# q's shift row folded and summed by one matmul, Wo split into two parts, and the third modulation vector applied behind Wo's product

## The chip, the cores and the metric

The kernel runs on one core of a Trainium2 chip. The metric is the device time of one execution in microseconds (us). The core has a matrix engine (TensorE, PE in the profile; its loads of weights have a row of their own, PEld), a vector engine (VectorE, DVE), an engine for activations and copies (ScalarE, ACT), GpSimd (POOL) and SyncE (SP), which here issues loads. Each engine works its own list of instructions in order, and engines wait for each other by semaphores.

## The reference

One transformer block with modulation vectors made from a condition `c`, over S = 2048 tokens of D = 448 channels, in fp32:

```python
mod = (_silu(c) @ w_mod).reshape(c.shape[0], 6, 1, -1)
sa, ca, ga, sb, cb, gb = (mod[:, 0], ..., mod[:, 5])
h = _layernorm(x, axis=-1) * (1 + ca) + sa
x = x + ga * _A_ref(h, A_wqkv, A_wo)
h = _layernorm(x, axis=-1) * (1 + cb) + sb
x = x + gb * _B_ref(h, B_w1, B_b1, B_w2, B_b2)
```

`_A_ref` is linear attention with 16 heads of 28 channels: q, k, v = h @ wqkv; phi(t) = where(t > 0, t + 1, exp(t)) + 1e-6 of q and k; kv = sum over tokens of phi(k) v, z = sum of phi(k); o = phi(q) kv / (phi(q) z + 1e-6); and the result is o @ wo. `_B_ref` is an MLP across the tokens (2048 to 1792 and back, gelu between), with a layer norm ahead of it.

`ga`, the third modulation vector (`mods[2]` in the code), scales the channels of what Wo puts out. So it may stand on Wo's columns, or on any product that ends with Wo.

## The kernel before

**Numbers.** Nearly every fp32 operand is split into a high part in a shorter format (fp32r) and a low part, the rest; a product of two is then three matmuls, high by high, low by high and high by low. Where the code splits, ACT makes the high part and DVE the low one by a subtraction (`split`), or ACT writes the negative of the high part and a transfer issued by POOL adds the full tile to it (`pkl` of most tiles, L527, and the later pieces of W1). A few matmuls take fp32 operands unsplit; the profile shows such a one as two records.

**Stage A, by token tiles t = 0 to 15 of 128 tokens (to some 98 us).** For each tile, PE projects k (`kp`, ten matmuls, L432) and closes it with one more matmul, whose operands are the rows of the layer norm's statistics (`hl`, made from `rw`, a transposition of the tile `rowst` that DVE fills, L395, L398, L404) and of the weights' column sums (`wrow`, L439). ACT takes exp and relu (`ek`, `rk`), DVE makes phi(k) (`pk`), and it is split into `pkh` and `pkl`; the normalised tile `xn` is split into `xh` and `xl`. Four tiles later (`KV_LAG`) PE adds the outer product of xn and phi(k) to four banks (`cacc`, eleven matmuls, L554). From t = 10 a projection of q (`qp`, with `eq`, `rq` and `pq`) comes with each tile. Past t = 15 the last four outer products follow, and two matmuls that sum phi(k) (`zp`, from `zh` and `zl`).

q needs a row of its own in `wrow`: the product of sa with the weights, `row_part` (DVE, into the tile `accb`), summed over its partitions together with the negative column sums of the scaled weights. `row_sum(0)` is seven matmuls, `row_bias(0)` the one for `accb`, in fp32; both stand at the start of t = 9, and `row_out(0)` at its end writes the sums into `wrow`.

**Between the stages (98 to 112 us).** From `cacc` and `zb`, a copy of zp, DVE and ACT make four tiles `cs`; PE multiplies them with v's weights (`kvb`), DVE applies the mask of the heads (`kvm`), and PE multiplies it with Wo in four groups of 112 rows (`wp`, fp32, L968). Wo's rows had been multiplied by `mods[2]` on DVE, one group each at the end of t = 13, 14 and 15 and one behind (L779, L791). ACT copies wp to `wpg`; transfers gather it into `wpr`, which is split into `wph` and `wpl`.

**Then i = 0 to 20.** For each tile, DVE makes 1 / den from phi(q) and zb and scales phi(q) to `pn` (L836 to L850); PE transposes it (`tq`), ACT and DVE split that, PE multiplies with wph and wpl (`op`), and the second layer norm follows. Five tiles later, PE adds the tile to the MLP's first layer (`up`, with W1 in pieces `pr`, each split into `ph` and `pl`). The first eight pieces are split by ACT and DVE, the others by ACT and a transfer (`PIECE_DMA`). The rest of the first layer and the second layer, `y`, run to the end.

**Order.** The order is written out by hand: each engine works its instructions as the code has them. Tiles come from a pool of 74 slots and another of 27 (`slot`, `tslot`), handed out in the order of the code, and one that takes a used slot waits until its last reader is done. Eight banks hold PE's results.

## Time and profile before

| | us |
|---|---|
| three runs | 433.62, 434.19, 433.53 (median 433.62) |
| the profiled execution | 434.09 |
| its span, first to last instruction | 432.4 |
| PE busy | 427.9 (99%) |
| DVE busy | 365.1 (84%) |
| ACT busy | 278.9 (65%) |
| POOL busy | 120.1 (28%) |

A row of the timeline gives the start and the length of an instruction in us, the engine, the line, the operation, what it writes and reads, and in brackets how long the engine had been idle before it and who ended that. Matmuls overlap: one is listed with 0.36 us, but in a row of them the next starts 0.20 us later. So PE's cost is read from the distance of starts, or from the chain of waits, where a run of matmuls of one line is one row.

### The profile page before, as it was taken

The numbers are of one execution on the slowest core, as the hardware profiler recorded it, in microseconds if no ns is written. First come the engines' busy times: TensorE is split into PE (matmuls) and PEld (weight loads), VectorE is DVE, ScalarE is ACT, GpSimd is POOL, SyncE is SP. The second block draws the span as 40 slices with busy tenths as digits, with TensorE's granted clock in tenths as the row PEclk, the third lists the DMA queues.
The fourth block names the chain that finished last, engine by engine and source line by source line (L and its number), as shares of the span: only waits on it lengthen the run. The fifth ranks groups of instructions, "written<-read, shape, count | busy, mean of one in ns | idle before, by whom it ended". The sixth has DMA issues, their size and how long they took to land.

```text
span 432.4 us, 7216 instructions
## 1 busy us (share of the span) xinstructions
PE 427.9 (99%) x2331; PEld 398.0 (92%) x2331; DVE 365.1 (84%) x814; ACT 278.9 (65%) x595; POOL 120.1 (28%) x199
## 2 busy tenths in 40 slices
PE   8999999999999999999999999999999999999997
PEld 8888899999899999999999999999999999999996
DVE  4899987889899999998579695739799998898894
ACT  5799869658578899996755263537464664655550
POOL 4345444300026577775200000010113131132010
PEclk9999999999999999999999999999999999999999
DMA  8997997565300036354427461577379977986431
GB/s 282 385 337 162 239 264 162 89 206 193 86 1 0 26 74 148 74 125 97 145 85 244 142 212 50 166 203 210 79 193 214 207 159 159 214 170 144 85 46 41
DMA packets 63797, 66.14 MB, mean 153 GB/s; under 512 B 4816, under 2 KB 55312, under 8 KB 63760
## 3 DMA queue, kind: packets, MB, share of 16 engines
q1 hardware_dynamic: 54688, 50.90, 37.8%
q0 software_dynamic: 8784, 14.32, 20.8%
q10 hardware_dynamic: 288, 0.46, 0.4%
q8 instruction: 18, 0.29, 0.3%
q14 instruction: 19, 0.16, 0.1%
HBM read 46.30 MB, written 7.34 MB: 124 GB/s over the span
## 4 chain that ended last, share of the span: by engine, by line
PE 97%; DVE 1%; ACT 1%; issue 0%
PE y L1183 19%; PE up L951 10%; PE up L950 10%; PE up L952 10%; PE y L1184 9%; PE cacc L554 7%; PE qp L432 7%; PE op L893 7%; PE kp L432 6%; PE op L900 1%; PE warm L188 1%; PE tq L863 1%; PE qp L439 1%; PE kvb L818 1%; PE wp L968 1%; PE rowb L287 1%
## 5 line engine op out<-in xcount | busy, mean ns | idle before, releaser
L950 PE MATMUL up<-h2h,ph 128*128 128x448 f32 x224 | 81.2, 362 | 0.0
L951 PE MATMUL up<-h2l,ph 128*128 128x448 f32 x224 | 81.2, 362 | 0.0
L952 PE MATMUL up<-h2h,pl 128*128 128x448 f32 x224 | 80.8, 361 | 0.0
L1138 POOL DMA_DIRECT2D a<-a x16 | 14.2, 964 | 142.6 <-DMA pr<-in_B_w_dram 76.7
L950 PEld LDWEIGHTS up<-h2h,ph 128*128 128x128 f32 x224 | 42.0, 188 | 3.1
L952 PEld LDWEIGHTS up<-h2h,pl 128*128 128x128 f32 x224 | 41.9, 187 | 3.0
L951 PEld LDWEIGHTS up<-h2l,ph 128*128 128x128 f32 x224 | 42.0, 188 | 2.3
L84 DVE TENSOR_TENSOR pl<-pr,ph 128x512 fp32r<-128x512 f32 x46 | 30.7, 688 | 2.6 <-ACT ph L83 1.7
L1189 ACT ACTIVATE cc<-y 128x448 f32<-128x448 f32 x24 | 13.0, 546 | 26.7 <-PE y L1184 26.7
L1102 DVE TENSOR_TENSOR u<-u,mod 128x448 f32<-128x448 f32 x14 | 8.7, 623 | 23.0 <-ACT u L1101 22.8
L83 ACT ACTIVATE ph<-pr 128x512 fp32r<-128x512 f32 x46 | 27.6, 623 | 0.8 <-PE up L952 0.5
L1101 ACT ACTIVATE u<-up,b 128x448 f32<-128x448 f32 x14 | 8.8, 625 | 25.4 <-PE up L952 24.9
L432 PE MATMUL kp<-wh,hh 128*128 128x448 f32 x64 | 23.8, 377 | 0.0
L554 PE MATMUL cacc<-pkh,xh 128*128 128x448 f32 x64 | 23.6, 369 | 0.0
L432 PE MATMUL qp<-wh,hh 128*128 128x448 f32 x64 | 23.5, 368 | 0.0
L1203 POOL DMA_DIRECT2D out_dram<-yt x14 | 12.7, 909 | 37.3 <-DVE yt L1194 27.9
L843 POOL TENSOR_SCALAR den<-den 128x16 f32<-128x16 f32 x16 | 8.8, 548 | 44.2 <-DVE den L840 44.2
L554 PE MATMUL cacc<-pkl,xh 128*128 128x448 f32 x56 | 20.3, 362 | 0.0
L893 PE MATMUL op<-wph,pth 128*128 128x448 f32 x48 | 18.7, 390 | 0.0
L1144 DVE TENSOR_TENSOR a<-a,s 128x512 f32<-128x512 f32 (+1 forms) x32 | 18.5, 622 | 0.0
L83 ACT ACTIVATE s2h<-s 128x512 fp32r<-128x512 f32 (+1 forms) x16 | 8.3, 569 | 15.5 <-DVE s L1144 15.5
L1183 PE MATMUL y<-ub,a11h 128*128 128x448 f32 x56 | 18.2, 375 | 0.0
(235 smaller groups left out, 1383.7 us busy)
## 6 DMA issues: line engine op xcount, KB each, us to landing
pr<-in_B_w_dram SPq DMA_DIRECT2D x56, 256.0 KB, 3.1
a<-in_B_w_dram SPq DMA_DIRECT2D x32, 256.0 KB, 4.8
a<-in_B_w_dram SPq DMA_DIRECT2D x32, 192.0 KB, 4.7
xt<-in_xt_dram SPq DMA_DIRECT2D x16, 256.0 KB, 5.0
x<-in_A_x_dram SPq DMA_DIRECT2D x16, 224.0 KB, 5.0
wm<-in_B_wmod_dram SPq DMA_DIRECT2D x16, 196.0 KB, 5.2
out_dram<-x SPq DMA_DIRECT2D x14, 224.0 KB, 2.3
out_dram<-yt POOLq DMA_DIRECT2D x14, 224.0 KB, 6.1
```

What stands on the lines that cost most here:

```text
L83: nc.scalar.activation(hi, full, AF.Copy)
L84: nc.vector.tensor_sub(lo, full, hi.bitcast(F32))
L432: nc.tensor.matmul(pps[t, j][:, :D], a[:, ch * P:(ch + 1) * P], w, start=first, stop=False)
L554: nc.tensor.matmul(cacc[ch][:, :D], a[:, s], b, start=(t == 0 and i == 0), stop=(t == NT - 1 and i == len(todo) - 1))
L893: nc.tensor.matmul(opb[t][:, :D], a, b, start=(ch == n == 0), stop=False)
L950: nc.tensor.matmul(ps[:, :D], hi[:, sl], mh, start=first, stop=False)
L951: nc.tensor.matmul(ps[:, :D], hi[:, sl], ml, start=False, stop=False)
L952: nc.tensor.matmul(ps[:, :D], lo[:, sl], mh, start=False, stop=last)
L1138: nc.gpsimd.dma_start(w, a, accum_op=ALU.add)
L1144: nc.vector.tensor_tensor(w, raw2[q, a][i], raw2[q, b][i], op=op)
L1183: nc.tensor.matmul(ps[:, :D], h[:, s], w, start=opens and r == 0, stop=False, skip_group_check=True)
L1184: nc.tensor.matmul(ps[:, :HD], l[:, s], wh, start=False, stop=closes and r == PAIRS - 1, skip_group_check=True)
```

## The change

**q's row.** At the end of `row_part` at t = 8, DVE adds the lower half of `accb`'s partitions to the upper (`row_fold`). At t = 9 ACT writes the high part of these 64 rows into a tile `rb`, and a copy of the selecting matrix in fp32r (`sel_r`); DVE writes the low part into rb's other 64 rows. `row_bias(0)` is then one fp32r matmul over all 128 rows. `row_sum(0)` and `row_bias(0)` move from the start of t = 9 to the start of t = 10, `row_out(0)` from the end of t = 9 to behind the closing matmul of t = 10. Three parts of `mods[2]` are spread over t = 7, 9, 10 and 11 instead of 7 to 10.

**Wo.** The four multiplications by `mods[2]` go. Each group of Wo is split by two ACT instructions and an adding transfer of POOL's (`wo_split`): two groups at the end of t = 13, one at the end of t = 14 and of t = 15. `kvm` is split by ACT and DVE, and `wp` is three matmuls for each group, twelve in all, in four banks. DVE multiplies each bank by `mods[2]` into `wpg`, where ACT copied it.

**What moves with it.** Pieces 6 and 7 of W1 are split by ACT and a transfer, at the end of i = 0, and pieces 4 and 5 behind kvm's split. The scaling of tile 0's phi(q) moves ahead, into the places where pieces were split.

On ACT, around the end of t = 14 and of t = 15, before (`pkh`, `xh` with the number of the token tile; eq4 and rq4 are q's fourth tile, ek15 and rk15 k's fifteenth, zh the high part of the sum of phi(k)):

```order
L515 ACTIVATE pkh13_1234<-pk13_1174 128x448
L500 ACTIVATE xh13_1241<-xn13_1239 128x448
L465 ACTIVATE eq4_1266<-qp4_1212,mv4_416 128x448
L466 ACTIVATE rq4_1267<-qp4_1212,mv4_416 128x448
L446 ACTIVATE ek15_1272<-kp15_1189,mv14_989 128x448
L449 ACTIVATE rk15_1273<-kp15_1189,mv14_989 128x448
L515 ACTIVATE pkh14_1276<-pk14_1245 128x448
L500 ACTIVATE xh14_1283<-xn14_1281 128x448
L500 ACTIVATE xh15_1290<-xn15_1288 128x448
L515 ACTIVATE pkh15_1302<-pk15_1286 128x448
```

and of the change, from xh13 on:

```order
L514 ACTIVATE xh13_1256<-xn13_1254 128x448
L698 ACTIVATE woh2_1264<-wo2_789 112x448
L699 ACTIVATE wol2_1265<-woh2_1264 112x448
L479 ACTIVATE eq4_1285<-qp4_1227,mv4_417 128x448
L480 ACTIVATE rq4_1286<-qp4_1227,mv4_417 128x448
L460 ACTIVATE ek15_1291<-kp15_1204,mv14_993 128x448
L463 ACTIVATE rk15_1292<-kp15_1204,mv14_993 128x448
L529 ACTIVATE pkh14_1295<-pk14_1260 128x448
L514 ACTIVATE xh14_1302<-xn14_1300 128x448
L514 ACTIVATE xh15_1309<-xn15_1307 128x448
L698 ACTIVATE woh3_1316<-wo3_791 112x448
L699 ACTIVATE wol3_1317<-woh3_1316 112x448
```

The pair for a group of Wo stands behind xh and ahead of the next eq, or of pkh15, which follows the last row; the two pairs of t = 13 stand in the same manner ahead of eq3.

On PE, at t = 9 and the start of t = 10, before (`rowb0` is q's row, `wh0` and `wl0` its weights, cacc5's operands are tile 5's):

```order
L439 MATMUL kp9_733<-wrow1_280,hl9_630 128x448
L287 MATMUL rowb0_806<-wh0_0_534,sel_s_100 98x448
...
L290 MATMUL rowb0_806<-accb0_561,sel_b_90 98x448
L554 MATMUL cacc0_437<-pkh5_632,xh5_701 128x448
...
L404 MATMUL rw10_826<-ident_78,rowst2_105 98x128
L432 MATMUL kp11_870<-wh1_0_222,hh11_762 128x448
```

and of the change:

```order
L453 MATMUL kp9_734<-wrow1_281,hl9_631 128x448
L568 MATMUL cacc0_438<-pkh5_633,xh5_702 128x448
...
L418 MATMUL rw10_818<-ident_78,rowst2_106 98x128
L290 MATMUL rowb0_864<-wh0_0_535,sel_s_100 98x448
...
L293 MATMUL rowb0_864<-rb0_829,sel_r_101 98x448
L446 MATMUL kp11_873<-wh1_0_223,hh11_764 128x448
```

The row's eight matmuls have changed places with tile 5's outer product and the transposition rw10, and the last of them reads rb0.

On DVE, between the stages, before:

```order
L470 SCALAR_TENSOR_TENSOR pq5_1428<-eq5_1424,rq5_1425 128x448
L84 TENSOR_TENSOR pl4_1443<-pr4_1312,ph4_1442 128x512
L84 TENSOR_TENSOR pl5_1447<-pr5_1314,ph5_1446 128x512
L470 SCALAR_TENSOR_TENSOR pq6_1473<-eq6_1469,rq6_1470 128x448
L822 TENSOR_TENSOR kvm_1475<-kvb_1452,mask_83 112x448
L84 TENSOR_TENSOR pl6_1486<-pr6_1316,ph6_1485 128x512
L84 TENSOR_TENSOR pl7_1490<-pr7_1318,ph7_1489 128x512
L836 SCALAR_TENSOR_TENSOR pd0_1505<-pq0_998,zb_1382 128x448
L840 TENSOR_REDUCE den0_1507<-pd0_1505 128x16
L846 RECIPROCAL den0_1507<-den0_1507 128x16
L850 SCALAR_TENSOR_TENSOR pn0_1511<-pq0_998,den0_1507 128x448
```

and of the change:

```order
L484 SCALAR_TENSOR_TENSOR pq5_1450<-eq5_1446,rq5_1447 128x448
L813 SCALAR_TENSOR_TENSOR pd0_1464<-pq0_1002,zb_1404 128x448
L817 TENSOR_REDUCE den0_1466<-pd0_1464 128x16
L484 SCALAR_TENSOR_TENSOR pq6_1492<-eq6_1488,rq6_1489 128x448
L823 RECIPROCAL den0_1466<-den0_1466 128x16
L876 TENSOR_TENSOR kvm_1497<-kvb_1471,mask_83 112x448
L827 SCALAR_TENSOR_TENSOR pn0_1499<-pq0_1002,den0_1466 128x448
L86 TENSOR_TENSOR kvl_1502<-kvm_1497,kvh_1501 112x448
L240 TENSOR_TENSOR acc3_1177<-acc3_1177 48x448
L86 TENSOR_TENSOR pl4_1525<-pr4_1335,ph4_1524 128x512
L1002 TENSOR_TENSOR wpg0_1544<-wp0_1528,mod2_1111 112x448
```

pd0, den0 and its reciprocal have come ahead of kvm, kvl and the products wpg behind it, and pl4 has gone from ahead of kvm to behind kvl.

The diff, without the functions b_prod to b_scale, which only stand earlier in the text:

```diff
-PIECE_DMA = range(8, 18)
+PIECE_DMA = range(6, 18)
+PARTS = (7, 9, 10)
+WO_AT = {13: (0, 1), 14: (2,), 15: (3,)}
...
-    cst.tile([P, 112], F32, name="space")
+    cst.tile([P, 14], F32, name="space")
...
+    sel_r = cst.tile([P, ROWS], F32R, name="sel_r")
...
     def row_bias(j):
-        nc.tensor.matmul(rowb[j][:ROWS, :D], sel_b, accb.pop(j), start=False, stop=True)
+        nc.tensor.matmul(rowb[j][:ROWS, :D], sel_r if j == 0 else sel_b, accb.pop(j), start=False, stop=True)
+
+    def row_fold(j):
+        acc = accb[j]
+        nc.vector.tensor_add(acc[:64], acc[:64], acc[64:])
+
+    def row_high(j):
+        acc, both = accb[j], moving(slot, f"rb{j}")
+        nc.scalar.activation(both[:64], acc[:64], AF.Copy)
+        nc.scalar.activation(sel_r, sel_b, AF.Copy)
+        accb[j] = both
+        return lambda: nc.vector.tensor_sub(both[64:], acc[:64], both[:64].bitcast(F32))
...
+    def wo_split(g):
+        full, hi, lo = wo_sb[g], moving(slot, f"woh{g}", parts=G), moving(slot, f"wol{g}", parts=G)
+        nc.scalar.activation(hi, full, AF.Copy)
+        nc.scalar.activation(lo, hi.bitcast(F32), AF.Copy, scale=-1.0)
+        nc.gpsimd.dma_start(lo, full, accum_op=ALU.add)
+        wos.append((hi, lo))
...
     for t in range(4, NT):
+        if t == 10:
+            row_sum(0)
+            row_bias(0)
         if 5 < t < NT - 1:
             project(t + 1, 1, "kp")
         kp = close(t, 1) if t > 4 else kps[4]
-        if t == 9:
-            row_sum(0)
-            row_bias(0)
+        if t == 10:
+            row_out(0)
         if t > 4:
             a_outer(t - KV_LAG)
...
             row_part(0, t - 5)
+            if t == 8:
+                row_fold(0)
         a_phi_q(t in Q_EARLY)
         if t == 9:
             a_exp(t, kp)
+            row_high(0)()
...
         if t == 11:
+            mod_part(2, 3)
+            mod_add(2)
             low2 = mod_high(2)
...
-        if t == 9:
-            row_out(0)
...
-        if 7 <= t < 11:
-            mod_part(2, t - 7)
-        if t == 10:
-            mod_add(2)
+        if t in PARTS:
+            mod_part(2, PARTS.index(t))
...
-        if t >= 13:
-            nc.vector.tensor_mul(wo_sb[t - 13], wo_sb[t - 13], mods[2][:G])
+        for g in WO_AT.get(t, ()):
+            wo_split(g)
         load_to(PRE_LOAD.get(t, 0))
...
     a_outer(NT - 3)
-    nc.vector.tensor_mul(wo_sb[3], wo_sb[3], mods[2][:G])
...
     a_q(late.pop(0))
-    split_to(6)
+    b_prod(0)
+    b_sum(0)
+    b_eps(0)
     mp = mod_sum2(4)
...
     a_phi_q()
+    b_recip(0)
+    mod_out(4, mp)
     kvm = slot("kvm", parts=G)
     nc.vector.tensor_mul(kvm, kvb[:G, :D], mask)
-    mod_out(4, mp)
+    b_scale(0)
+    kvh, kvl = slot("kvh", dt=F32R, parts=G), slot("kvl", dt=F32R, parts=G)
+    split(kvm, kvh, kvl)
     load_to(PRE + MID + 3)
-    split_to(8)
...
     a_q(late.pop(0))
-    for fn in (b_prod, b_sum, b_eps, b_recip, b_scale):
-        fn(0)
     mod_add(3)
+    split_to(5)
+    wps = [bank(f"wp{g}") for g in range(4)]
+    for gs in ((0, 1), (2,), (3,)):
+        for i, (a, b) in enumerate(((kvh, 0), (kvh, 1), (kvl, 0))):
+            for g in gs:
+                nc.tensor.matmul(wps[g][:G, :D], a[:, g * G:(g + 1) * G], wos[g][b], start=(i == 0), stop=(i == 2))
     for g in range(4):
-        wp = bank(f"wp{g}")
-        nc.tensor.matmul(wp[:G, :D], kvm[:, g * G:(g + 1) * G], wo_sb[g], start=True, stop=True)
         wpg = tslot(f"wpg{g}", parts=G)
-        nc.scalar.activation(wpg, wp[:G, :D], AF.Copy)
+        nc.vector.tensor_mul(wpg, wps[g][:G, :D], mods[2][:G])
...
     low3 = mod_high(3)
+    split_to(6)
```

43 lines of the change are left out of this document (22 added, 21 removed).

## The prediction

> **What bounds the kernel now.** I read the cores' spans and clocks first, then the page's busy times, then who makes TensorE (PE) wait (us in total, times, longest), then the chain that ended last (start, us, what).
>
> ```profile
> core 0: 432.4 us, clock 1.000
> PE 427.9 (99%) x2331; PEld 398.0 (92%) x2331; DVE 365.1 (84%) x814; ACT 278.9 (65%) x595; POOL 120.1 (28%) x199
> PE warm L188 <- DVE roots L108: 1.1, 1, 1.1
> PE rw L404 <- ACT rk L449: 0.2, 1, 0.2
> 53.56 2.01 PE kp L432 x10
> 51.23 2.22 PE cacc L554 x11
> 50.48 0.75 PE rowb L290 x2
> 108.81 3.01 PE wp L968 x8
> ```
>
> PE is busy for 99% of the span and waits for other engines only twice, 1.3 us in all. It is the bound, and it is fed with little to spare: whatever PE issues less is gained, and whatever reaches PE late is lost, since no later wait exists that could take the loss back. So the change has two sides: what PE no longer does, and what now comes too late. Averages say nothing of the second: ACT is busy for 65% only, but what counts is where in its order the new work stands.
>
> **What PE saves.** Matmuls that follow one another issue every 0.20 us (ten take 2.01, eleven 2.22). The bias matmul of the row now takes 0.75 in two passes and becomes one of the common kind: -0.55. Wo's four products take 3.01 in eight records, and twelve common matmuls take 12 x 0.20 = 2.4: -0.6. If nothing came late, the sum would be -1.15.
>
> **Place A, the row (t = 8 to 10): +0.85 net.** Before, seven sums and the bias stand ahead of tile 5's outer products; afterwards they stand behind those and the transposition rw. VectorE (DVE) has this there:
>
> ```profile
> 49.01 0.69 DVE L280 SCALAR_TENSOR_TENSOR accb<-wr,col,accb 128x448 f32<-128x448 f32 x1
> 49.61 0.51 DVE L496 TENSOR_SCALAR xn<-x,mv 128x448 f32<-128x448 f32 x1
> 50.64 0.16 DVE L398 TENSOR_TENSOR rowst<-mv,rowst 128x4 fp32r<-128x4 f32 x1
> 51.92 0.68 DVE L232 SCALAR_TENSOR_TENSOR acc<-wm,sc,acc 112x448 f32<-112x448 f32 x1
> 52.51 0.62 DVE L380 BATCH_NORM_STATS2 st<-x 128x6 f32<-128x448 f32 x1
> 53.27 0.48 DVE L496 TENSOR_SCALAR xn<-x,mv 128x448 f32<-128x448 f32 x1
> 61.72 0.62 DVE L237 TENSOR_TENSOR acc<-acc 48x448 f32<-48x448 f32 x1
> 62.26 0.62 DVE L380 BATCH_NORM_STATS2 st<-x 128x6 f32<-128x448 f32 x1
> 48.70 0.36 PE L439 MATMUL kp<-wrow,hl 98*128 98x448 f32 x1
> 53.29 0.27 PE L404 MATMUL rw<-ident,rowst 128*98 128x128 f32 x1
> 53.60 0.36 PE L432 MATMUL kp<-wl,hh 128*128 128x448 f32 x1
> ```
>
> The fold has no row; the nearest is L237, the same kind of in-place add, after which the next instruction starts 0.54 later. Here it waits for accb (49.01 + 0.69) and starts at some 49.73, the next at 50.27 instead of 49.61: +0.66. So rowst, which rw reads, ends at 51.47 instead of 50.80. PE comes to rw at 48.90 + 11 x 0.20 = 51.11 instead of 53.29, and waits some 0.45. The seven sums then issue until 53.07. The low half of the folded row is made by DVE ahead of xn. The part of a modulation vector at 51.92 has left this place (-0.59), so xn's old 53.27 becomes 53.35, and the low half, a subtraction as long as L237, ends at 53.97. The bias matmul can issue at 54.05, 0.95 late, and the projection behind it at 54.25 where it stood at 53.40 (the row of 53.60 less one matmul). +0.85 holds the 0.55 saved. Bounds: -0.55 if DVE's slack were there after all, +1.2 if the fold takes its full 0.62 and 0.2 more for each wait.
>
> **Place C, Wo's parts (t = 13 to 15): +2.8.** This is the costliest. ScalarE (ACT) and DVE hand tiles to and fro:
>
> ```profile
> 78.37 0.57 ACT L407 ACTIVATE hl<-rw 34x128 fp32r<-34x128 f32 x2 [2.94 <-PE rw L404]
> 80.01 0.58 ACT L515 ACTIVATE pkh<-pk 128x448 fp32r<-128x448 f32 x1
> 80.62 0.58 ACT L527 ACTIVATE pkl<-pkh 128x448 fp32r<-128x448 f32 x1
> 81.11 1.03 ACT L500 ACTIVATE xh<-xn 128x448 fp32r<-128x448 f32 x2
> 82.50 0.62 ACT L465 ACTIVATE eq<-qp,mv 128x448 f32<-128x448 f32 x1
> 84.57 0.58 ACT L515 ACTIVATE pkh<-pk 128x448 fp32r<-128x448 f32 x1
> 85.18 0.63 DVE L525 SCALAR_TENSOR_TENSOR pkl<-pk,pkh 128x448 fp32r<-128x448 f32 x1 [0.88 <-ACT pkh L515]
> 86.80 0.58 ACT L500 ACTIVATE xh<-xn 128x448 fp32r<-128x448 f32 x1 [1.65 <-DVE xn L496]
> 87.28 0.62 ACT L465 ACTIVATE eq<-qp,mv 128x448 f32<-128x448 f32 x1
> 91.66 0.58 ACT L500 ACTIVATE xh<-xn 128x448 fp32r<-128x448 f32 x1 [1.71 <-DVE xn L496]
> 92.57 0.55 DVE L506 TENSOR_TENSOR xl<-xn,xh 128x384 fp32r<-128x384 f32 x1
> 93.86 0.36 PE L554 MATMUL cacc<-pkh,xh 128*128 128x448 f32 x1
> 96.89 0.63 DVE L84 TENSOR_TENSOR zl<-pk,zh 128x448 fp32r<-128x448 f32 x1 [0.70 <-ACT zh L83]
> ```
>
> ACT starts when PE has made rw (78.37) and runs without a gap to pkh at 84.57; DVE makes pkl, a sum and xn from there; ACT makes xh and starts the next tile's eq. From eq to eq it takes 4.78 us, and ACT's idle times of 1.65 and 1.71 lie inside, between pkh and xh. Wo's parts stand behind xh and ahead of eq, so they cannot use those gaps: they lengthen the loop. The four multiplications that DVE loses (0.54 each) shorten nothing, since DVE waits for ACT in it (0.88).
>
> One part is two ACT instructions, the second reading the first, as pkh and pkl: 0.61 + 0.49 = 1.10. Two parts come at the end of t = 13 (+2.20), one behind xh of t = 14 (+1.10), one ahead of the last pkh (+1.10). So tile 14's xh ends at 92.24 + 3.30 = 95.54. The outer products of tile 14, due at 93.86, start at 95.66: +1.8. Their third matmul reads xl, which follows xh by one subtraction (92.57 + 0.55 + 3.3 = 96.43): another 0.53. Then pkh and pkl of tile 15, late by 4.4 and by some 3.7, cost 0.16 at the second matmul of tile 15, and zl, made from the sum of all pk behind them, 0.3 at the last matmul of zp. 1.8 + 0.53 + 0.16 + 0.3 = 2.8. Bounds: with 0.49 an instruction tile 14's xh is 2.94 late and the sum 2.0; with pkl and the sums behind DVE's queue it is 3.5.
>
> **Place B, from zp to the first tq: +0.4 instead of -0.6.** Let Z be the end of zp (98.82 before).
>
> ```profile
> 98.42 0.40 PE zp L799 x2
> 104.08 0.62 DVE L470 SCALAR_TENSOR_TENSOR pq<-eq,rq 128x448 f32<-128x448 f32 x1
> 106.68 0.63 DVE L822 TENSOR_TENSOR kvm<-kvb,mask 112x448 f32<-112x448 f32 x1 [0.24 <-issue]
> 107.22 1.28 DVE L84 TENSOR_TENSOR pl<-pr,ph 128x512 fp32r<-128x512 f32 x2
> ```
>
> Before, kvm starts at Z + 7.86, and wp follows at Z + 9.83. Afterwards the scaling of tile 0 (pd, den, its reciprocal) stands ahead of kvm, and two halves of kvm, on ACT and DVE, behind it. The changed program's waits also show the four cs tiles taking slots that the two projections of q before them read to the end, which holds eq back by over 1 us. Step by step: pq at Z + 7.0, reciprocal at 9.2, kvm 9.4 to 10.05, pn, then kvh until 10.6 and kvl until 11.25. wp is due at Z + 10.15 (0.3 lost to the late cs) and starts at 10.8; with 2.4 the first tq comes at Z + 13.2, before at 12.83. Bounds: -0.6 with everything in time, +1.0 if the reciprocal's hand-over to POOL and back takes another 0.6.
>
> **Place D, tiles 1 to 5 behind it: +0.6.** Here DVE scales pn just ahead of PE's transposition:
>
> ```profile
> 120.21 0.56 DVE L878 TENSOR_TENSOR ptl<-tq,pth 128x384 fp32r<-128x384 f32 x1 [0.20 <-ACT pth L874]
> 137.05 0.62 DVE L850 SCALAR_TENSOR_TENSOR pn<-pq,den 128x448 f32<-128x448 f32 x1
> 138.20 0.44 PE tq L863 x4
> 145.52 0.62 DVE L909 SCALAR_TENSOR_TENSOR x<-op,x 128x448 f32<-128x448 f32 x1 [0.44 <-PE op L900]
> ```
>
> pn, as the fourth tile shows, ends 0.53 ahead of it. DVE gains four multiplications by the modulation vector (wpg, 0.54 each) and kvl, and loses the low halves of pieces 6 and 7 (1.28): 5 x 0.54 less 1.28 leaves it some 1.4 us further behind PE. Bounds 0, if earlier idle time takes it up, and +0.9 (1.4 less 0.53, if nothing does); I take 0.6, nearer the second, as DVE has no idle time between 120.21 and 145.52. The same two pieces give ACT four instructions, some 2.2 us, after Wo's last high half; their POOL transfers and the loads that wait for released slots have until the first up matmul, tens of us later: nothing, and the loss of a piece's delay if a slot were refused that long.
>
> **The sum.** 0.85 + 2.8 + 0.4 + 0.6 = +4.65. The profiled execution took 434.09 us, its span being 432.4 with 1.7 around it, so it would become 438.7. The median of the three runs is 433.62, 0.47 lower: 438.3.
>
> **Rivals.**
> 1. It does what it says, and the slack holds: -1.15, 432.5 us. For it: PE is the bound, and ACT idles 35% of the span. Against: the gaps lie inside the loop, not at Wo's place. Chance 0.10.
> 2. It comes out even: C is hidden, A costs its 0.85, B gains 0.6: 433.9. For it: 2.94 us of idle ACT ahead of t = 13's work. Against: that idle time ends with PE's own rw, and cannot be used ahead. Chance 0.07.
> 3. Slower, but by the loop alone: A and B gain their 0.55 and 0.6, D nothing, C costs 2.8: +1.65, 435.3. It decides as soon as ACT's added time before tile 14 exceeds the 1.62 between xh's end and 93.86. For it: A, B and D rest on margins under 1 us. Chance 0.15.
> 4. PE's clock falls in the pauses of C and recovers behind them. If each matmul took twice its 0.20 over the 22 of tiles 14 and 15 (4.4 us) that would add 4.4; over 40% of them, some 1.7: 440.0. Against: the granted clock is 1.000 in the run shown, with a pause of 1.1 at its start. Chance 0.06. The Trainium skill, "TensorE: Matmul & The Clock Gate", Part 1, "What's actually happening", has the clock halved after at least one idle window of about 3.4 us and restored after a busy one; by that rule C's longest pause, 1.8, is too short, and no run shown here holds one that is long enough.
>
> **The numbers.** The forecast, 438.3, has the other 0.62. Its own range is 436.0 to 440.2: from 2.0 in C with A's first wait (0.45) hidden and nothing in B and D (2.4 in all), to C 3.5 with A, B and D at their upper bounds (6.6). For 8 in 10 the range reaches down over part of rival 3, to 434.8, and leaves rivals 1 and 2 out. A difference below 0.2% (0.87 us) cannot be told from none here: faster is rival 1, 0.10; the same is rival 2, 0.07; slower has 0.83.
>
> **What will show it.** In the list of PE's waits, which holds only 1.3 us now, there should stand: cacc for ACT's xh and DVE's xl, some 2.3; rowb for DVE's rb, 0.95; rw for DVE's rowst, 0.45; wp for DVE's kvl; tq for DVE's pn. eq to eq should be 5.9 us instead of 4.78 between tiles 3 and 4. The bias matmul should be one record of 0.2, and wp twelve. If cacc shows no wait, place C is wrong, and the time falls to 436 or less; if the waits are there but the time is below 434, PE must have saved more than the 1.15.

## The result, and the profile after

The changed kernel takes 444.89 us (median of six runs, 442.98 to 445.08) against 433.82 before: the ratio is 1.0243, 95% interval 1.0221 to 1.0264. It is slower, as forecast, but by 11 us and not by 4.65, and above the range that was given. The six runs fall into two groups that only the granted clock tells apart: 443.22 and 442.98 with a mean clock of 1.000, and four of 444.87 to 445.08 with 0.996. The profiled execution is that of 443.22.

The page of the changed kernel, and the list of what PE waited for (us in total, times, longest), which held 1.3 us before:

```profile
span 441.5 us, 7245 instructions
PE 431.6 (98%) x2334; PEld 394.9 (89%) x2334; DVE 366.0 (83%) x815; ACT 284.7 (64%) x604; POOL 126.9 (29%) x205
PE cacc L568 <- ACT xh L514: 2.0, 1, 2.0
PE rowb L293 <- DVE rb L304: 1.0, 1, 1.0
PE wp L999 <- ACT kvh L85: 0.6, 1, 0.6
PE tq L893 <- DVE pn L827: 0.5, 2, 0.2
PE modp L256 <- DVE mh L246: 0.4, 1, 0.4
PE kvb L870 <- DVE cs L859: 0.3, 1, 0.3
PE cacc L568 <- DVE xl L520: 0.2, 1, 0.2
PE rw L418 <- DVE rowst L412: 0.2, 1, 0.2
```

The waits that the prediction named are there, nearly at the forecast size, and the waits listed add up to some 5 us. (wp waits for ACT's kvh and not, as the forecast's list of signs had it, for DVE's kvl.) But PE is also *busy* for 3.7 us longer (431.6 against 427.9), with work that was meant to shrink by 1.15. That part is in no list of waits. Much of it shows when the same ten matmuls are compared in the two chains of waits (start, us, what), the kernel before first, where two projections of q follow zp:

```profile
98.82 2.00 PE qp L432 x10
101.02 2.00 PE qp L432 x10
```

and the changed one:

```profile
103.67 2.05 PE qp L446 x10
105.93 2.06 PE qp L446 x10
```

Each matmul of k, of q, and of the attention's output issues 0.2055 us after the last one instead of 0.2005; those of cacc and up keep their 0.20.

Cut into stages at PE's own milestones, with the view that sums each stretch (window and its length; the busy time and instructions of PE, PEld, DVE, ACT and POOL; the granted clock, the DMA share and GB/s), before:

```profile
46.70:53.30 6.60, 6.60 (x33) 5.55 (x32) 6.46 (x19) 5.05 (x10) 4.79 (x5) 1.00 1.09 246
53.30:87.25 33.95, 33.95 (x172) 31.58 (x171) 27.71 (x61) 24.77 (x50) 13.18 (x15) 1.00 0.77 176
87.25:98.66 11.41, 11.41 (x59) 10.69 (x57) 10.30 (x22) 5.94 (x12) 0.00 (x0) 1.00 0.63 205
98.66:111.65 12.99, 12.99 (x75) 10.90 (x74) 12.21 (x21) 9.93 (x19) 0.29 (x1) 1.00 0.40 137
111.65:142.50 30.85, 30.85 (x165) 28.75 (x163) 28.56 (x65) 23.07 (x53) 10.50 (x21) 1.00 0.10 29
```

and after:

```profile
46.20:54.00 7.80, 6.62 (x32) 5.27 (x31) 7.57 (x20) 7.07 (x16) 4.64 (x5) 1.00 1.09 254
54.00:88.90 34.90, 34.51 (x170) 31.42 (x169) 25.43 (x56) 24.70 (x50) 15.30 (x17) 1.00 0.71 154
88.90:103.50 14.60, 12.44 (x58) 10.38 (x57) 10.66 (x22) 8.97 (x18) 1.67 (x2) 1.00 0.77 188
103.50:117.40 13.90, 13.09 (x80) 11.58 (x79) 11.95 (x22) 8.74 (x17) 0.57 (x1) 1.00 0.52 170
117.40:150.40 33.00, 32.30 (x164) 28.44 (x163) 30.44 (x69) 24.79 (x56) 12.64 (x23) 1.00 0.19 44
```

The stages are: kp10 to kp11 (place A), from there to tile 11's outer product, the last five outer products and zp (place C), to the first tq (B), to the first up matmul (D). They grew by 1.2, 1.0, 3.2, 0.9 and 2.2. The rest of the kernel grew by 1.2, and the start was 0.5 shorter. That makes the 9.1 between the two spans.

### The profile page after: what moved, and what is told of

Read it like the earlier page. It is cut to its first block, busy times and chain, and to the rows that moved or that the text cites. A ratio compares the mean times of both kernels' runs of the same rounds, so it can differ in the third digit from the quotient of the medians.

```text
span 441.5 us, 7245 instructions
## 1 busy us (share of the span) xinstructions
PE 431.6 (98%) x2334; PEld 394.9 (89%) x2334; DVE 366.0 (83%) x815; ACT 284.7 (64%) x604; POOL 126.9 (29%) x205
## 4 chain that ended last, share of the span: by engine, by line
PE 72%; DVE 13%; DMA 5%; ACT 4%; issue 2%; POOL 1%; SPq 1%; DVEq 0%; ACTq 0%
PE y L1216 18%; PE up L980 10%; PE up L982 10%; PE up L981 10%; PE y L1217 9%; PE op L923 6%; DMA pk<-pk 2%; PE qp L446 2%; PE cacc L568 1%; PE tq L893 1%; PE op L930 1%; DVE xn L510 1%; DVE st L394 1%; DMA wt<-in_first_dram 1%; DVE hl L429 1%
## 5 line engine op out<-in xcount | busy, mean ns | idle before, releaser
L86 DVE TENSOR_TENSOR pl<-pr,ph 128x512 fp32r<-128x512 f32 x44 | 29.5, 686 | 2.7 <-ACT ph L85 1.7
L85 ACT ACTIVATE ph<-pr 128x512 fp32r<-128x512 f32 x44 | 26.4, 618 | 0.8 <-PE up L982 0.5
L1236 POOL DMA_DIRECT2D out_dram<-yt x14 | 12.7, 909 | 40.0 <-DVE yt L1227 30.5
```

The source lines that it names most:

```text
L85: nc.scalar.activation(hi, full, AF.Copy)
L86: nc.vector.tensor_sub(lo, full, hi.bitcast(F32))
```

## The experiments

**The address of the smaller pool.** The diff shortens a tile called space, from 112 to 14 columns, and adds sel_r with 98. In bytes that is even (448), but each tile is rounded up to a multiple of 32, and 64 + 416 is 480. So every tile of the smaller pool starts 32 bytes further on in the changed program, no longer at a multiple of 64. (These are the program's addresses; the profile shows none.) Two runs move only that. The first shortens the pad of the changed kernel:

```diff
-    cst.tile([P, 14], F32, name="space")
+    cst.tile([P, 6], F32, name="space")
```

> The changed kernel with its pad tile 32 bytes shorter, so that the tiles of the smaller pool start at multiples of 64 bytes again, as they did before the change; nothing else differs. Theory (address): in the profiles the matmuls that stream a tile of that pool issue every 0.2055 us after the change and every 0.2005 before, 0.005 us more on 528 matmuls of k, q and the attention's output, and some 0.5 us in the last stage; so this kernel takes 2.6 to 3.1 us less than the changed one, 440.2 at the full clock. Rival: the distance between the matmuls comes from something else (traffic of transfers, the pauses), and the time stays at 443 to 445.

Measured: 442.1 (four runs, 441.39 to 443.56), ratio to before 1.0204, interval 1.0185 to 1.0222. The matmuls are back at 0.20 (a run of ten q matmuls takes 2.00). The gain is 2.0 in the means (444.3 to 442.3). At a clock of 1.000 it is 443.1 to 441.6, at 0.996 some 2. That is the direction of the theory, at less than its size (2.6 to 3.1).

The second lengthens that of the kernel before:

```diff
-    cst.tile([P, 112], F32, name="space")
+    cst.tile([P, 120], F32, name="space")
```

> The kernel before with its pad tile 32 bytes longer; nothing else differs. Theory (address): the same 0.005 us on each of the 528 matmuls and some 0.5 in the last stage, here without any wait: 2.6 to 3.1 us slower than before, 436.5 to 436.9, the matmuls of kp, qp and op 0.2055 us apart. Rival: no difference to the kernel before, 433.8.

Measured: 435.94, ratio 1.0061 (1.0048 to 1.0073), 2.5 us slower with no wait added anywhere. From kp10 to the end the profile gives 2.5, and another 0.4 from the first row sums to kp10; what lies ahead of those was 1.0 shorter in this execution. Its chain has the figures of the changed kernel:

```profile
57.48 2.05 PE qp L432 x10
59.74 2.05 PE kp L432 x10
61.99 2.22 PE cacc L554 x11
```

So 32 bytes of padding are worth some 2.5 us here: the tiles that lie in the smaller pool stream more slowly, and cacc's, from the larger pool, which did not move, do not. All runs below have the old addresses; where that takes another pad, the diffs leave its line out.

**Each half alone.** First the kernel before with the row's hunks of the change, and no others:

```diff
+        if t == 10:
+            row_sum(0)
+            row_bias(0)
...
+            if t == 8:
+                row_fold(0)
...
+            row_high(0)()
...
+        if t in (7, 9, 10):
+            mod_part(2, (7, 9, 10).index(t))
```

> The kernel before with q's row folded and summed as in the change, at the old addresses, without the change of Wo and without what moves with it. Theory of the prediction (place A alone): 0.85 us slower than before, with waits of PE for the row's low half (1.0) and for rowst (0.2 to 0.45). Rival: the time that the row's matmul saves is kept (-0.55), or a tile that the pool now hands out in another order waits for an adding transfer and costs more than 1.5.

Measured: 435.96, ratio 1.0051 (1.0037 to 1.0065), 2.5 us slower. kp10 to kp11 takes 7.85 instead of 6.61 (+1.24), and PE waits a second time, for the low part of the modulation vector at t = 12 (+0.68 from there to tile 11's outer product). That is 1.9 of the 2.0 us between the two profiles. The reason stands further up, on ACT and DVE, where the tiles eq of q's first token tile and xn of tile 11 wait for a transfer:

```profile
64.46 0.64 ACT L477 ACTIVATE eq<-qp,mv 128x448 f32<-128x448 f32 x1 [4.14 <-DMA pk<-pk]
68.29 0.51 DVE L508 TENSOR_SCALAR xn<-x,mv 128x448 f32<-128x448 f32 x1 [2.02 <-DMA pk<-pk]
75.41 0.44 PE L254 MATMUL modp<-mh,ones_r 128*128 128x448 f32 x1 [0.61 <-DVE mh L244]
```

A tile waits until the last reader of its slot is done. By the program's hand-out of slots, which no view shows, these slots held phi(k) of tiles 8 and 10, which an adding transfer reads: the one that xn waits for was issued at 60.81 and landed 7.4 us later. In the kernel before, by the same hand-out, eq had the slot of a tile of the modulation vector's weights (wm), which had been free for long; it has no such wait there.

Then the changed kernel with these hunks taken back:

```diff
-        if t == 10:
-            row_sum(0)
-            row_bias(0)
...
+        if t == 9:
+            row_sum(0)
+            row_bias(0)
...
-        if t in PARTS:
-            mod_part(2, PARTS.index(t))
+        if 7 <= t < 11:
+            mod_part(2, t - 7)
```

> The changed kernel with q's row as before, at the old addresses: only Wo's parts, the twelve matmuls, the vector applied behind them and the moved pieces. Theory of the prediction (places B, C, D without A): 3.8 us slower than before, 437.6. By the changed kernel's profile, where C cost 3.2, B 0.9 and D about 2, it is some 5.5 to 6 slower, 439.5. Rival: ScalarE's loop at t = 13 to 15 matters only together with the row's delay, and the time is within 1.5 us of before.

Measured: 441.43, ratio 1.0184 (1.0169 to 1.0199): 8.0 us slower, where 3.8 had been the prediction's and 5.5 to 6 the profile's. Wo's half is by far the larger. The halves do not add up: 2.5 and 8.0 against 8.7 for the whole change at the old addresses. PE's pauses in its profile are C's (1.5 and 0.2) and a longer one, 2.2, at op behind the first tq, where the profile names ACT's rq, which stands with pth behind the pieces' four instructions. But those were late themselves in this run: ahead of them ACT waited for the last of the transfers that gather wpr, one of which took 4.2 us to land. In the changed kernel none took more than 2.6, and the same wait was 0.76.

```profile
124.00 0.58 ACT L85 ACTIVATE wph<-wpr 128x448 fp32r<-128x448 f32 x1 [2.66 <-DMA wpr<-wpg]
```

So some 1.9 of the 2.2 are the transfer's; why it was late is open. Behind that pause the matmuls are 0.37 us apart for some 2.5 us, and all four runs have a mean clock of 0.996, so the 8.0 hold a stretch at the lower clock.

**Place C.** First Wo's parts are made earlier:

```diff
-WO_AT = {13: (0, 1), 14: (2,), 15: (3,)}
+WO_AT = {10: (0, 1), 12: (2, 3)}
```

> The changed kernel at the old addresses, with Wo's parts made at the end of t = 10 (two groups) and t = 12 (two) instead of t = 13 to 15. Theory of the prediction (place C is ScalarE's loop): ScalarE idles 3.4 and 2.9 us at t = 11 and 13 of the kernel before, so that 2.2 us fit there; the pauses of PE at the outer products of tile 14 (2.1 and 0.2) go, and with them the lower clock behind them: 438 to 439 instead of 441.6. Rival (slots): the eight tiles are then held longer, other tiles wait for their slots, and the time stays within 1 us of 441.6, with waits at other places. Rival: the loop is slow by something else, and PE still waits some 2 us for xh of tile 14.

Measured: 440.25, ratio 1.0154 (1.0138 to 1.0169). Tile 14's wait for xh is gone and C takes 11.9 instead of 15.7 with the lower clock. But PE waits 1.9 for rq of q at t = 11: the parts now stand ahead of eq and rq there, whose bank PE needs. And ACT's idle time was not theirs to use:

```profile
63.76 0.58 ACT L698 ACTIVATE woh<-wo 112x448 fp32r<-112x448 f32 x1 [4.12 <-issue]
```

The first part starts only after 4.12 us for which the profile names no releaser. In the run with the pad put right, eq waits 4.46 at this place for an adding transfer of phi(k); so a late slot is the likely cause, and Wo's four instructions come on top of it. I had counted ACT's idle time, and neither what it waits for nor who waits for what stands behind. The clock held (0.999 to 1.000).

Then the parts stay at their places, but DVE makes the low ones:

```diff
-        nc.scalar.activation(lo, hi.bitcast(F32), AF.Copy, scale=-1.0)
-        nc.gpsimd.dma_start(lo, full, accum_op=ALU.add)
+        nc.vector.tensor_sub(lo, full, hi.bitcast(F32))
```

> The changed kernel at the old addresses, with Wo's low parts made by VectorE (a subtraction in the place where the kernel before multiplied) instead of ScalarE and an adding transfer; the high parts stay at their places on ScalarE. Theory of the prediction (each ScalarE instruction in the loop lengthens it): two instructions per tile become one, so that the loop grows by 0.5 and not 1.1 a tile and PE's pause at tile 14 falls from 2.1 to about 0.5: 440 instead of 441.6, and the clock should hold. Rival: VectorE's 0.54 each lengthen the loop by as much, no difference.

Measured: 439.66, ratio 1.0140 (1.0125 to 1.0155), the clock 1.000 in all four runs. The loop answers as the theory says. From eq to eq it took 4.78 us before, 5.88 with two instructions of Wo's in it (changed kernel), and 5.29 with one:

```profile
86.76 0.62 ACT L479 ACTIVATE eq<-qp,mv 128x448 f32<-128x448 f32 x1
91.56 0.56 ACT L698 ACTIVATE woh<-wo 112x448 fp32r<-112x448 f32 x1
92.15 0.58 ACT L699 ACTIVATE wol<-woh 112x448 fp32r<-112x448 f32 x1
92.64 0.61 ACT L479 ACTIVATE eq<-qp,mv 128x448 f32<-128x448 f32 x1
```

```profile
86.14 0.61 ACT L479 ACTIVATE eq<-qp,mv 128x448 f32<-128x448 f32 x1
90.97 0.56 ACT L698 ACTIVATE woh<-wo 112x448 fp32r<-112x448 f32 x1
91.43 0.62 ACT L479 ACTIVATE eq<-qp,mv 128x448 f32<-128x448 f32 x1
```

(the first fence is the changed kernel's, the second this run's). PE's wait for xh fell from 2.1 to 0.3.

**Place D.**

```diff
-        split_to(8 + max(0, i - 5))
+        split_to(6 if i < 4 else 8 + max(0, i - 5))
```

> The changed kernel at the old addresses, with the split of W1's pieces 6 and 7 put off from the end of i = 0 to the end of i = 4. Theory (place D is those four ScalarE instructions, 2.4 us ahead of tile 1's pth and of the next eq and rq, whose banks PE waits for): from the first tq to the first up matmul the changed kernel took 2.2 us more than the kernel before; some 1.5 of it go, 440.0 instead of 441.6. Rival of the prediction (D is VectorE's four multiplications by the vector): the time stays at 441.6 within 0.5 us.

Measured: 442.88, ratio 1.0210 (1.0190 to 1.0230); at the full clock 441.62, so no gain at all. The stages say why: from the first tq to the first up matmul it takes 31.75 instead of 32.7 (D falls by 1.0, and what is left is PE's wait for pn, 0.9), and from there to the end 1.0 more. At the new place the chain of waits leads from the four instructions over eq, rq and DVE's pq, which waits 1.18 for rq, to pn, for which PE then waits 0.6. The four ACT instructions cost a microsecond where they stand, and a microsecond at the one other place that was tried.

**Both costs taken away.** The run with Wo's half alone, and both of these edits:

```diff
-WO_AT = {13: (0, 1), 14: (2,), 15: (3,)}
+WO_AT = {10: (0, 1), 12: (2, 3)}
...
-        split_to(8 + max(0, i - 5))
+        split_to(6 if i < 4 else 8 + max(0, i - 5))
```

> The row as before, the old addresses, Wo's parts at the end of t = 10 and 12, and W1's pieces 6 and 7 split at the end of i = 4: the change of Wo with both of the costs taken away that the theory names. Theory: places A, C and D cost nothing, and B stays between -0.6 and +0.9: 433.0 to 434.8, against 433.4 of the kernel before and 441.4 of the change of Wo alone. Rival: the cost lies in the slots and in the late cs, kvm and wpg as well, and it stays above 436.

Measured: 441.11, ratio 1.0174 (1.0157 to 1.0191): a clear miss. PE waits 1.3 for rq in stage A, 0.6 for kvh, 1.2 for op's last part and 1.2 for pn, while C is gone. For the most part, moving the instructions moved the wait. The 1.2 at op is another thing: no piece stands ahead of pth there any more, but ACT waits 2.60 for the last gathering transfer of wpr, which took 4.1 us as in the run with Wo's half alone.

**Slots.** For the row, first a run that takes no slot more: rb goes into a tile that nothing uses after t = 1 (it is made wide enough for that; the rest is the row's half as above).

```diff
-        acc, both = accb[j], moving(slot, f"rb{j}")
+        acc, both = accb[j], junk
```

> The row's change alone, as in the run that had only that (435.96), but the split row is written into a tile that nothing uses after the second token tile, so that the pool hands out no slot more and every later tile has the slot that it had before the change. Theory (the row costs twice: PE waits for its low half, 1.25 us at tile 10, and the one slot more makes eq and xn wait for the adding transfers of the sums of phi(k), which delays the low part of a modulation vector and holds PE for 0.6 us more): the waits of ScalarE and VectorE for these transfers go, PE no longer waits for that part, and the time is 434.8 to 435.3. Rival: the late modulation vector is late because its parts were spread out to t = 11; then PE's wait of 0.6 stays, and the time is 435.9.

Measured: 435.17, ratio 1.0034 (1.0022 to 1.0046). eq still waits for the transfer, 5.1 us, and xn 1.7; PE waits 0.4 for the vector and 0.9 for rq. So the theory fell in the form that I had written down: it is not the one slot more that deals eq a late slot. What is left is that the parts of the vector, moved from t = 8 to 11, give their own slots back later, so that eq takes another; no run moves these parts alone.

Then two slots more, for the row alone, the whole change, the whole change with Wo's low parts by DVE, and the kernel before:

```diff
-NSLOT, NTOK = 74, 27
+NSLOT, NTOK = 76, 27
```

> The row's change alone, with 76 slots in the pool instead of 74 (the memory has room for two more). With 74, eq of q's first tile took the slot of tile 8's phi(k), which an adding transfer reads until about 64 us, and xn of tile 11 waited likewise; with the tile junk instead of a new one it did so as well, since the parts of the modulation vector give their slots back later. Theory (slots): with two more, both take slots that were free long before; ScalarE's wait of 4 us and VectorE's of 2 go, PE's wait for the low part of the modulation vector (0.6) goes, and 435.2 to 435.9 becomes 434.7, place A's 1.25 alone. Rival: PE still waits 0.4 to 0.6 for it, since its parts are made later, and the time does not move.

> The whole change at the old addresses with 76 slots instead of 74. Theory (slots are part of A's and B's cost): PE's wait for the modulation vector's low part goes (0.4 to 0.7), cs waits one projection less, B falls from 0.8 to about 0.4; C and D stay: 440.4 to 440.7 at the full clock against 441.4 to 441.9, and up to 1.5 more where the clock falls in C. Rival: no difference.

> The same with 76 slots, and Wo's low parts by VectorE (with 74 slots that gave 439.7). Theory: the gains add up, since they lie at different places: 438.6 to 439.0. Rival (hidden): what the slots free is lost again at the next wait, 439.7.

> The kernel before with 76 slots instead of 74 and nothing else, as a control for the runs with 76. Theory (slots matter only where a tile waits for one): the kernel before waits for no slot that PE feels, so it stays within 0.3 us of 433.9, and the 2.0 us that the changed kernel gains by two slots are waits that the change brought. Rival: two slots more make every version faster, and this one by 1 us or more.

Measured: the row alone 435.35 (1.0032, 1.0020 to 1.0044); the whole change 440.08 (1.0150, 1.0130 to 1.0170); with Wo's low parts by DVE 437.64 (1.0090, 1.0075 to 1.0104). The last two gain 2.0 each by two slots. In the last, PE no longer waits for the vector, C takes 12.0 instead of 12.7 and B 12.8 instead of 13.8. The row alone missed its 434.7. The waits of eq, of xn and for the vector are gone, as the theory has it, but another has come: the bias matmul waits 1.7 instead of 1.0, since DVE, ahead of the row's low half, now waits for an adding transfer. (The profile names ACT's pkh; but the low half ended at 54.62, and PE started at 54.77.)

```profile
51.92 0.69 DVE L427 TENSOR_TENSOR hl<-xt,hh 128x512 fp32r<-128x512 f32 x1 [0.60 <-DMA pk<-pk]
```

And the control turns the reading round: the kernel *before* becomes slower with 76 slots, 435.34 (1.0043, 1.0029 to 1.0057), by one new wait, for the vector's low part at t = 12.

```profile
PE modp L253 <- DVE mh L243: 1.6, 1, 1.6
```

DVE's first part of another modulation vector waits 5.88 us ahead of it, and the chain of waits leads to an adding transfer of phi(k) that took 7.0 us (2.6 us more, behind its landing, have no name). So more slots do not help as such. With every tile that is added, or given back at another time, the slots are dealt anew, and each deal has a late slot somewhere or none. The 74 of the kernel before are a deal without one that PE feels. Part of the 2.0 is therefore waits which the change had brought by its own deal (the vector's low part, and cs), but I cannot name the share, since a deal cannot be changed at one place alone.

**The twelve matmuls by themselves.** Three runs start from the kernel before: Wo is multiplied by the vector on DVE as before, ACT copies wp as before, pieces 6 and 7 stay with ACT and DVE, and come behind tile 0's scaling. Only kvm's and Wo's halves and the matmuls are added. In the first, the halves of Wo lie in the larger pool and GpSimd makes the low ones:

```diff
+        if t == 12:
+            for g in range(4):
+                woh.append(moving(slot, f"woh{g}", parts=G))
+                wo_r.append(moving(slot, f"wol{g}", parts=G))
...
+        nc.scalar.activation(woh[g], wo_sb[g], AF.Copy)
+        nc.gpsimd.tensor_sub(wo_r[g], wo_sb[g], woh[g].bitcast(F32))
```

> The kernel before with Wo's product in twelve short matmuls and as little else as possible: VectorE multiplies Wo by the modulation vector as before; the high parts are made by ScalarE in its idle 2.6 us behind the last pkh, the low parts by GpSimd; ScalarE copies wp as before; W1's pieces 6 and 7 stay with ScalarE and VectorE and come behind the scaling of tile 0. Theory: nothing stands in ScalarE's loop (C), nor ahead of tile 1's pth (D), and of B only the wait for the split kvm is left: PE gains the 0.6 of the product, less up to 0.3, 432.8 to 433.2 against 433.4 before. Rival: the nine slots more make the cs tiles wait as in the changed kernel, and B's 0.8 stays: 434.2; or the split of kvm alone costs PE as much as it saves: 433.4.

Measured: 437.06, ratio 1.0080 (1.0066 to 1.0094), PE waiting 1.6 for cs. From the first tq to the first up matmul it is 1.9 slower, too, with one transfer of wpr landing 3.6 us after its issue. In the second they lie in the smaller pool, where k's weights have been given back by then:

```diff
-                woh.append(moving(slot, f"woh{g}", parts=G))
-                wo_r.append(moving(slot, f"wol{g}", parts=G))
...
+    for g in range(4):
+        woh.append(moving(tslot, f"woh{g}", parts=G))
+        wo_r.append(moving(tslot, f"wol{g}", parts=G))
     a_pk_parts(NT - 1)
```

> The kernel before with Wo's product in twelve matmuls and little else, as in the run that took 437.06, but the eight tiles of Wo's parts come from the smaller pool, where k's weights have been given back by then; so the 74 slots are handed out up to cs as they were before. That run lost 1.6 at kvb waiting for cs and 2.8 behind the first tq. Theory (slots): the wait of kvb for cs goes, the halves of Wo cost nothing, PE saves 0.6 and loses up to 0.5 waiting for the high half of kvm: 433.0 to 433.5 against 433.4 to 433.8; at best a little under the kernel before. Rival: GpSimd's subtractions beside VectorE slow VectorE down and kvb still comes late: 435 or more.

Measured: 435.60, ratio 1.0039 (1.0027 to 1.0051). The slots of cs are the old ones, and still PE waits 1.6 for cs. So my theory of the slots was wrong for this wait. The timeline shows the cause: DVE's instructions beside GpSimd's take more than twice their 0.62.

```profile
94.38 5.31 POOL L812 TENSOR_TENSOR wol<-wo,woh 112x448 fp32r<-112x448 f32 x3 [10.82 <-ACT woh L811]
95.72 1.45 DVE L818 TENSOR_TENSOR pk<-pk,pk 128x448 f32<-128x448 f32 x1
98.60 1.57 DVE L827 TENSOR_TENSOR wo<-wo,mod 112x448 f32<-112x448 f32 x1
100.86 4.03 POOL L812 TENSOR_TENSOR wol<-wo,woh 112x448 fp32r<-112x448 f32 x1 [1.18 <-ACT woh L811]
103.82 3.34 DVE L846 SCALAR_TENSOR_TENSOR cs<-zb,col,cs 128x448 f32<-128x448 f32 x4
```

The third gives the low parts back to ACT and a transfer, and moves Wo's fourth multiplication ahead of zl:

```diff
-        nc.gpsimd.tensor_sub(wo_r[g], wo_sb[g], woh[g].bitcast(F32))
+        nc.scalar.activation(wo_r[g], woh[g].bitcast(F32), AF.Copy, scale=-1.0)
+        nc.gpsimd.dma_start(wo_r[g], wo_sb[g], accum_op=ALU.add)
```

> As the run before with Wo's parts in the smaller pool (435.6), but the low parts by ScalarE's negative and an adding transfer instead of GpSimd's subtraction, and Wo's fourth multiplication ahead of zl, where VectorE idled 0.7 us. In that run kvb waited 1.6 us for cs, while VectorE's instructions beside GpSimd's took up to 2.3 times as long (1.45 and 1.57 instead of 0.62). Theory (the two engines slow each other): without the subtractions VectorE's instructions take 0.62 again, kvb no longer waits, and the saving of the twelve matmuls shows: 433.2 to 433.7 against 433.9 before, in the run's own comparison 0.2 to 0.7 us faster or no difference. Rival: ScalarE's eight instructions now delay zh and zb, and kvb still waits a us: 435.

Measured: 433.40 (twelve runs, 432.96 to 434.99) against 433.54, ratio 1.0001 (0.9991 to 1.0011). No difference, at the upper end of what was expected. All waits of the two runs before are gone. These are two edits at once, and no run parts them; but the rows show what the first one did. In its chain of waits, kvb follows the projections without a gap:

```profile
102.70 0.21 PE modp L253
102.91 3.14 PE kvb L856 x32
108.28 2.46 PE wp L986 x12
```

DVE's sum of phi(k) takes 0.62 again, and the four cs 2.47 instead of 3.34. wp takes 2.46 instead of 3.01, and from the end of zp to the first tq it is 12.45 instead of 12.99: the 0.54 that were promised. Behind it, tiles 1 to 5 take 31.16 instead of 30.85. So the product alone saves PE half a microsecond, and a third of one is given back. No version found here beats the kernel before.

## Why the prediction was right or wrong

**The direction, and why,** were right: PE has no wait to lose, the added ACT work stands inside ACT's loop with DVE, and PE pays for it at tile 14. The size was less than half, and three steps of the prediction failed. It had no term for the address of the smaller pool (2.5 us). It put the four ACT instructions of pieces 6 and 7 at nothing (1.0 in place D). And it left the lower clock out of the sum as a rival with a chance of 0.06 (1.8 in four of six runs). The terms of A, B and C were the right ones, each too small by 0.3 to 0.5, and in A a second wait of 0.6 was not seen. Step by step, from the profile at the full clock:

| step | predicted | measured |
|---|---|---|
| A, kp10 to kp11 | +0.85 | +1.2 |
| A, later: the vector's low part at t = 12 | none | +0.6 |
| C, the outer products and zp | +2.8 | +3.2 |
| B, zp to the first tq | +0.4 | +0.9 |
| D, tq to up | +0.6 | +2.2 (0.3 to 0.6 of it address) |
| the smaller pool's address | none | 2.5, of which 1.6 lie outside the rows above |
| the clock in C's pauses | rival 4, 440.0 | +1.8 in four of six runs |

**The address** is the step that was missing altogether. I wrote down nothing for the pad tile, since 14 and 98 columns add up to 112. What the shift costs could be seen in no row of the profile before, but that the tiles move could: the changed program can be built, and its addresses compared.

**A.** The bias matmul waited 1.0 for the low half and rw 0.2 to 0.3, by the list of waits. That list counts from the end of the matmul before, which is listed with 0.37, while the next would have started after 0.20; and one more distance behind each stop is 0.1 too long. So a stop costs PE some 0.3 more than its listed wait. By the starts, rw came 0.4 late (predicted 0.45) and the bias matmul 1.1 (0.95), each with 0.1 behind it, and the row's matmul saved 0.5. The prediction's upper bound for A, 1.2, adds up to 1.3 from its own terms. The second wait came from moving the parts of the vector. The prediction booked that move as relief for DVE (-0.59). It did not ask what these parts hold: their slots, and a term that PE needs at t = 12.

**C.** The mechanism is shown, by the loop's 4.78, 5.29 and 5.88 us and by PE's wait of 2.0 at tile 14. By the starts, with what each stop costs behind it, tile 14's first outer product was 2.2 late (predicted 1.8), its third 0.5 (0.53), tile 15's second 0.2 (0.16) and the end of zp 0.3 (0.3): only the first term was too small. Against ACT's start in this stage, xh of tile 14 came 3.8 later and not 3.3, since ACT also waited 0.4 for xn ahead of Wo's parts.

**B.** kvb waited 0.3 for cs (predicted 0.3) and took 3.6 instead of 3.1, wp waited 0.6 for kvh (0.65) and cost 0.8 with its restart, wp itself saved 0.5, and the address added 0.1: +0.9. The steps were right, the sum was too small by the restarts behind kvb's and wp's stops.

**D.** The prediction looked at DVE (wpg, kvl) and got its part right: what was left when the pieces were moved is 0.9, at PE's wait for pn. It called the two pieces' four ACT instructions free, "tens of us later". They stand ahead of pth and of three pairs of eq and rq, and delay them by 2.4 (the first and the last of the four are shown):

```profile
124.90 0.61 ACT L340 ACTIVATE ph<-pr 128x512 fp32r<-128x512 f32 x1
126.73 0.63 ACT L341 ACTIVATE pl<-ph 128x512 fp32r<-128x512 f32 x1
127.27 0.47 ACT L901 ACTIVATE pth<-tq 128x384 fp32r<-128x384 f32 x1
129.40 0.44 PE L930 MATMUL op<-wph,pth 128*128 128x448 f32 x1 [0.19 <-ACT rq L480]
```

What an instruction costs is not when its own result is needed, but what stands behind it on its engine.

**The rivals.** 1 and 2 are out. 3 (the loop alone) is out, since A, B and D all cost. 4, given 0.06, happened in four of the six runs of the changed kernel, at about its price: 1.7 in the forecast, 1.8 between the two groups. The profile of the run with the pad put right shows it, with PE's stop of 2.1 and the matmuls behind it 0.37 us apart, until they are 0.20 apart again:

```profile
98.63 0.47 PE L568 MATMUL cacc<-pkh,xh 128*128 128x448 f32 x1 [2.09 <-ACT xh L514]
100.44 0.57 PE L568 MATMUL cacc<-pkl,xh 128*128 128x448 f32 x1
100.81 0.57 PE L568 MATMUL cacc<-pkh,xl 128*128 128x448 f32 x1
```

That is 1.5 us in this execution. The changed kernel's own profile has a stop of 2.0, and the distance stays 0.20. The record of the granted clock in the traces tells them apart. In all 18 profiles of this case it changes only at whole multiples of 3.41 us after its first rise. On this grid, the stretch with the stop and the one behind it are, in the run with the pad put right (columns as in the stages above: PE's busy time is the second number behind the window, the granted clock the third from the end):

```profile
95.89:99.31 3.42, 1.33 (x6) 0.57 (x4) 2.98 (x7) 1.39 (x3) 0.00 (x0) 1.00 0.77 194
99.31:102.72 3.41, 3.20 (x10) 2.85 (x10) 2.49 (x6) 1.68 (x4) 0.83 (x1) 0.50 0.82 246
```

and in the changed kernel, where the stop lies across an edge of the grid:

```profile
93.46:96.87 3.41, 2.22 (x12) 1.74 (x10) 2.17 (x5) 1.83 (x4) 0.46 (x1) 1.00 0.53 79
96.87:100.29 3.42, 2.45 (x11) 1.96 (x12) 2.53 (x8) 2.67 (x5) 0.33 (x1) 1.00 0.86 289
```

Four profiles have a fall (the pad put right, Wo's half alone, the pieces put off, the whole change with 76 slots). In each the clock is 0.50 for one stretch of 3.41 us, and in the stretch ahead of it PE was busy for 1.21 to 1.69 us. In every other stretch of the grid in the 18 profiles, the last 20 us of each span left out, PE was busy for 1.75 us or more, and the clock stayed. So the length of a stop does not decide alone: 1.4 us brought the fall with 76 slots, 2.0 did not in the changed kernel. Where the grid begins differs from run to run (4.0 to 10.6 us from the start of the span), so it is luck whether a run is caught. The Trainium skill, "TensorE: Matmul & The Clock Gate", "What's actually happening", asks for an idle window of about 3.4 us before the clock halves, and says that the window runs freely. The traces agree with the length and fit a window that runs freely; but it need not be idle, for PE was busy in 1.33 of the 3.41 us above. The pause of 1.1 that the prediction held against this rival lies ahead of the first record of the clock, and says nothing about it.

## What to carry to other kernels

Where one engine never waits, an average of idle time elsewhere says nothing: ask which loop the new instruction stands in, and who waits for what stands behind it. Before forecasting, build both programs and compare which addresses and which slots the tiles get, for a pad of 32 bytes and a slot given back later were worth more here than the matmuls saved. A saving of half a microsecond on the bounding engine is real only if making its operands touches neither.

## What was not expected of the hardware

- The start of a streamed operand matters: 0.2055 us a matmul of 448 columns instead of 0.2005 when the tile starts 32 bytes further on, by the program's addresses 32 past a multiple of 64 (two kernels with, the others without, and cacc's tiles unmoved as a control in each).
- The clock fell for 3.41 us where PE was busy for 1.69 us or less of one stretch of a grid of 3.41 us, and at no busier stretch (18 profiles): a pause of 1.4 us can be enough, and one of 2.0 can pass.
- GpSimd beside VectorE: three subtractions of 112 by 448 took 5.31 us, and a VectorE addition of 0.62 took 1.45 meanwhile. The Trainium skill, "SBUF — State Buffer", section "SBUF: two separate sides", has the two engines share one pair of ports that one holds for a whole instruction; the row agrees that they hinder each other.
- The adding transfers of phi(k) landed between 3.2 and 8.2 us after their issue (in the kernel before and the two runs of the row alone with 74 slots), so a slot that waits for one can be twice as late as another.
- The first row sums start between 14.5 and 15.9 us in the profiles, with the same code up to there. In the kernel before, the fourteen warming matmuls took 3.0 us, in the changed one 1.6: the record of the clock begins at 10.0 us in the one and at 4.7 in the other. How soon the clock rises differs from run to run, and may explain part of the scatter of 1 us.
